# An attention block and a squared-ReLU feed-forward layer on one core: loads of the first pair reordered, transposes of the last queries in other PSUM banks, sums of W_in one step later

## The chip, the core and the metric

The kernel runs on one core of one Trainium2 chip. The metric is device time in microseconds of one execution. The times given are medians of several executions; the profile is of one execution, taken by the hardware profiler.

The engines are named as in the profile: PE is TensorE (PEld its weight loads), DVE is VectorE, ACT is ScalarE, POOL is GpSimd, and SP is the engine that issues nearly all DMAs here.

## The reference

```python
# q, k, v: (8, 8, 576, 64) float32; g_norm: (64,)
kv = np.einsum('bhsd,bhse->bhde', k, v)
out = np.einsum('bhsd,bhde->bhse', q, kv)
rms = np.sqrt(np.mean(out * out, axis=-1, keepdims=True) + 1e-06)
attn = out / rms * g_norm                      # (B, H, S, D)
x = attn.transpose(0, 2, 1, 3).reshape(4608, 512)
h = x @ w_in                                   # w_in: (512, 2048) float64
g = np.maximum(h, 0.0) ** 2
return (g @ w_out).astype(np.float32)          # w_out: (2048, 512) float64
```

The attention is linear: a key-value matrix of 64 x 64 for each batch and head, a product with the queries, a normalization per head. Then come an up product, relu squared, and a down product.

## The kernel before

**Tiling.** A batch b has 576 tokens of 8 heads. Heads go in pairs p = 0 to 3, so that a pair fills 128 columns. The tokens of a batch are four blocks of 128 (C = 4) and a rest of 64; the rests of two batches share one tile, so two batches make nine tiles of 128 tokens (PAIR). 36 tiles form nine strips s of four tiles (512 tokens). For each strip the kernel makes x, transposed (features on the partitions, `xt`), multiplies it by W_in (`up`), squares, and multiplies by W_out (`down`).

**Attention.** `load(b, p)` fetches k, v and q of a pair, `load_rest` the last 64 keys and values of all heads of a batch (k_rest, v_rest), `load_q_rest` the last queries. `key_value` (L347) multiplies keys by values into a PSUM tile kv_ps and copies two 64 x 64 blocks to SBUF with ACT (L357, L358). Its last two products take k_rest and v_rest. `transposed_query` (L322) makes qT: for b = 0 and 1 with PE transposes (L335) and a copy by ACT (L337), for later batches with DVE. For b = 1 it also transposes the last queries (L342) and copies them (L345). `query` multiplies qT by the key-value blocks (L386, x_ps), `normalized` scales (L427), and `features` transposes the result with PE (L473) for b < 2; later batches use DVE and DMAs. For b = 0 the first four tiles go another way: `first_queries` (L436), `first_normalized` (L443), `first_features` (L460), pair by pair, as soon as a pair has been loaded.

**Weights.** W_in and W_out come as float64 in 32 raw pieces of 512 KB (`load_piece`, L192, eight buffers). ACT takes the two halves of the words apart (L204, L207), DVE puts float32 together (L216 to L225). From the second strip on, the products use fewer, larger combinations of quarters (a scheme of seven products for a 2 x 2 block matrix), so sums of weights are needed: `sums_in(g)` scales a quarter of W_in by g_norm with ACT (L251, 128 x 2048) and makes four sums with DVE (L253, L242); `sums_out` does the like for W_out, and its results are stored to DRAM.

**Order.** All of it is written out by hand; each engine runs its instructions in program order. The opening is the list `slices` up to `ready[0]`: for each pair of b = 0 transposes T, key-values K, first queries Q, normalization N and features F, with raw pieces 0 to 3 converted in between. Then come, in strip 0, 16 steps `up_first` (i = 0 to 15, eight matmuls of 512 columns each), before each of which `convert(5 + (3*i + 2)//4)` emits conversions; in the last eight steps one slice of b = 1 follows each (T(1,0), K(1,0), T(1,1), ... K(1,3)). After them come 14 steps `down` (i = n_up to n_up + 13, p in the order 1, 2, 5, 6, 7, 3, 4, two steps each); the second of each pair ends with `combine`: for p = 1, 5, 6 ACT copies the bank (snap, L586), for p = 2, 7, 3 DVE adds bank and snap (L714), for p = 4 ACT copies the result (L712). Then strip 1 begins.

**Buffers.** PSUM has a pool with tag "at" (two banks: kv_ps, xt_ps) and tag "x" (one tile of two banks: t_ps, x_ps), and a pool with tags A (two banks), B and C (one each) for the up and down products. Before the change the transposed last queries lie in the second half of the kv_ps tile of the same pair (`kv_places`), so `key_value` of (1, p) writes to the bank from which L345 copies. q, k and v have two buffers each.

The order of loads at the start, as SP issues it before the change: k_rest, v_rest of b = 0; then for each pair k, v, q (q in two DMAs), with one raw piece after each pair from the second on; then more raw pieces. k_rest and v_rest are first cleared by DVE (L292, L293).

Of the kernel before, what the change touches and what calls it, by code (L numbers as in the profile page):

```python
# [10 lines left out]
FP32 = mybir.dt.float32  # L11
# [9 lines left out]
def kernel(  # L21
# [34 lines left out]
    nc = tc.nc  # L56
    P = 128
    B, H, S, D = q.shape
# [5 lines left out]
    C = S // P  # L64
# [32 lines left out]

    def load(b, p, q_eng):
        hs = slice(2 * p, 2 * p + 2)
        if b == 0 and p >= 2:  # L100

            h_place = g_pool.tile([P, 4, C * P], FP32, name="first_qkv", tag="gt")
        for i, (n, src, eng) in enumerate((("k", k, nc.sync), ("v", v, nc.sync), ("q", q, q_eng))):
            whole = src[b, hs, 0 : C * P].rearrange("h (sp c) d -> sp h c d", c=C)
            if n == "q" and b >= Q_ON_PE:

                t = qkv_pool.tile([P, 4 * C, SQ], FP32, name=n, tag=n)
                for a in range(4):
                    h, f = divmod(a * SQ, D)
                    eng.dma_start(  # L110
                        out=t[ts(a, SQ)],
                        in_=src[b, 2 * p + h, 0 : C * P, f : f + SQ].rearrange("(i k) f -> i k f", k=4 * C),
                    )
            elif n != "q":
                if b == 0 and p >= 2:
                    t = h_place[:, i].rearrange("p (h c d) -> p h c d", h=2, c=C)
                else:
                    t = qkv_pool.tile([P, 2, C, D], FP32, name=n, tag=n)
                eng.dma_start(out=t, in_=whole)
            else:  # L120

                if b == 0 and p >= 2:
                    t = h_place[:, i].rearrange("p (c h d) -> p c h d", h=2, c=C)
                else:
                    t = qkv_pool.tile([P, C, 2, D], FP32, name=n, tag=n)
                for h in range(2):
                    eng.dma_start(out=t[:, :, h, :], in_=whole[:, h])
            main[n, b, p] = t
# [9 lines left out]
    def load_rest(b, eng):  # L138
        h = b % 2
        half = slice(REST * h, REST * (h + 1))  # L140
        for t, src in ((k_rest[half], k), (v_rest[half, h], v)):
            eng.dma_start(out=t, in_=src[b, :, C * P : S].rearrange("h s d -> s h d"))
# [20 lines left out]
    def load_next(q_eng=nc.sync):  # L163
        u = next(to_load, None)
        if u is not None:
            load(*u, q_eng)
# [82 lines left out]
    def sums_in(g):  # L249

        nc.scalar.activation(w_in[:, :, g, 0:4], w_in[:, :, g, 0:4], AF.Copy, scale=g_col)  # L251
        a11, a21, a12, a22, s1, s2, s4 = (w_in[:, :, g, b] for b in range(7))
        nc.vector.tensor_tensor(out=s1, in0=a21, in1=a22, op=ALU.add)  # L253
        minus(nc.vector, s2, s1, a11)
        minus(nc.vector, s4, a12, s2)
        minus(nc.vector, a21, a11, a21)
# [39 lines left out]
    nc.vector.memset(one, 1.0)  # L296
    nc.scalar.sqrt(one, one)

    load_rest(0, nc.sync)
    load_next()  # L300
    for p in range(1, NP):
        load_next()
        load_piece()
# [13 lines left out]
            qT["rest", b // 2, p] = t[:, p]  # L317
        return t

    kv_places = {}  # L320

    def transposed_query(b, p):  # L322
        t = main.pop(("q", b, p))
        if b >= Q_ON_PE:
            qT[b, p] = qt_pool.tile([P, C, P], FP32, name="qT", tag="qT")
            nc.vector.transpose(out=flat(qT[b, p]), in_=flat(t))
            if b % 2 and p == NP - 1:
                nc.vector.transpose(
                    out=open_rest(b).rearrange("p q (k t) -> p q k t", k=4),
                    in_=squares(q_rest[b // 2]).rearrange("p k q f -> p q k f"),  # L330
                )
            return
        ps = apsum.tile([P, 2, C, P], FP32, name="t_ps", tag="x", bufs=1)[:, 0]
        for c in range(C):
            nc.tensor.transpose(ps[:, c, :], flat(t[:, c]), ident)  # L335
        qT[b, p] = qt_pool.tile([P, C, P], FP32, name="qT", tag="qT")
        nc.scalar.copy(qT[b, p], ps)  # L337
        if b % 2:
            t = q_rest[b // 2][:, 2 * p : 2 * p + 2]
            kv_places[b, p] = apsum.tile([P, 2 * P], FP32, name="kv_ps", tag="at")  # L340
            ps = kv_places[b, p][:, P : 2 * P]
            nc.tensor.transpose(ps, flat(t), ident)  # L342
            if p == 0:
                open_rest(b)
            nc.scalar.copy(qT["rest", b // 2, p], ps)  # L345

    def key_value(b, p):  # L347
        tk, tv = main.pop(("k", b, p)), main.pop(("v", b, p))

        place = kv_places.pop((b, p), None) or apsum.tile([P, 2 * P], FP32, name="kv_ps", tag="at")  # L350
        ps = place[:, 0:D]
        for c in range(C + 1):
            for h in range(2):
                a, w = (tk[:, h, c, :], tv[:, h, c, :]) if c < C else (k_rest[:, 2 * p + h], v_rest[:, b % 2, 2 * p + h])
                nc.tensor.matmul(ps[ts(h, D)], lhsT=a, rhs=w, start=c == 0, stop=c == C)  # L355
        d = kv_all[:, (NP * b + p) % (2 * NP + 1)]
        nc.scalar.copy(d[0:D, 0:D], ps[0:D])  # L357
        nc.scalar.copy(d[D:P, D:P], ps[D:P])  # L358
        kvd[b, p] = d
        if b < 2:  # L360
            if b == 1 and p < 2:
                load_next()
        else:
            load_next()
            if p == NP - 1 and b + 1 < B:
                load_rest(b + 1, nc.sync)
                load_q_rest(b + 1, nc.sync)
# [460 lines left out]
    for s in range(N_STRIP):  # L828
        attend(ready[s])
        if s == 0:  # L830
            steps = [(2, up_first, (g, fh, i)) for g in range(NG) for fh in range(2) for i in range(2)]
        else:
            steps = [(1, up, (s, g, p)) for g in range(NG) for p in ORDER]
        n_up = len(steps)
        if s < DEEP:

            steps += [(2, down, (s, p, i)) for p in (ORDER if s else (1, 2, 5, 6, 7, 3, 4)) for i in range(2)]
        else:
            steps += [(2, down_deep, (s, k, i)) for k in range(7) for i in range(2)]
        goal = ready.get(s + 1, len(slices))  # L840
        total, done = sum(w for w, _, _ in steps), 0
        for i, (w, fn, a) in enumerate(steps):
            if s == 0 and i < n_up:

                convert(5 + (3 * i + 2) // 4)
                if i in (2, 4):
                    load_next()
                if i == 3:
                    load_q_rest(0, nc.sync)
                    load_rest(1, nc.sync)  # L850
                    load_q_rest(1, nc.sync)
            elif s == 0 and i == n_up:
                convert(len(conversions))
                conv.close()
                sum_pool = ctx.enter_context(tc.tile_pool(name="sum", bufs=8, reuse_waits="tile"))
                c_pool = ctx.enter_context(tc.tile_pool(name="c", bufs=6, reuse_waits="tile"))
                stream_pool = ctx.enter_context(tc.tile_pool(name="stream", bufs=4, reuse_waits="tile"))
                stream(3)
                for b, t in enumerate(w_first):
                    for e in range(2):  # L860
                        nc.sync.dma_start(out=w_out[b, :, e], in_=t[:, :, ts(e, P)])
            if s == 0 and n_up <= i < n_up + NG:
                sums_g(0, i - n_up)
            fn(*a)
            done += w
            if s:
                attend(ready[s] + int((goal - ready[s]) * min(done / (0.42 * total), 1)))
                if s >= DEEP and i == n_up - 3:
                    leaf_sums(s, 4)
                if s == DEEP - 1 and i == len(steps) - 1:  # L870
                    sums_x(s + 1)
                    stream(4)
                continue
            if i in (n_up + 4, n_up + 5):
                load_next()
            if i == n_up + 6:
                load_rest(2, nc.sync)
                load_q_rest(2, nc.sync)
            if i - n_up in (6, 8, 10, 12):
                sums_in((i - n_up - 6) // 2)  # L880
            if i == n_up + 9:
                sums_x(1)

            n_kv = ready[0] + 2 * NP
            if i < n_up:
                attend(ready[0] + max(0, (i + 1) - n_up + 2 * NP))
            else:
                attend(n_kv + (goal - n_kv) * min(i + 1 - n_up, 6) // 6)
# [30 lines left out]
```

## Time and profile before

| what | us |
|---|---|
| median of 5 runs | 949.53 (947.12 to 950.23) |
| the five runs | 947.5, 947.12, 950.23, 949.61, 949.53 |
| profiled execution | 947.5, span 945.7 |
| PE busy in 0 to 35 us | 17.57 |
| PE busy in 35 to 68.6 us | 33.57 of 33.60 |
| PE busy in 68.6 to 98.9 us | 27.57 of 30.30 |
| PE busy in 98.9 to 152.6 us | 53.02 of 53.70 |
| PE busy in 152.6 to 260 us | 104.03 of 107.40 |
| PE busy in 260 to 946 us | 680.36 of 686.00 |

How to read it: the span is the time from the first to the last instruction in the trace. "Busy" is the time in which an engine runs an instruction. A row of the timeline gives start, duration, engine, line, operation, written and read tiles with their shapes; in square brackets stand the idle time of the engine just before it and what ended that idle time. A row of waits gives the waiting engine and line, the releaser, the total in us, the number of waits and the longest. PEclk is the granted PE clock, 1.00 being full speed. In the first 35 us PE works half of the time; from there to the end it is busy almost without a break.

### The profile page before, as it was taken

The numbers are of one execution on the slowest core, as the hardware profiler recorded it, in microseconds if no ns is written. First come the engines' busy times: TensorE is split into PE (matmuls) and PEld (weight loads), VectorE is DVE, ScalarE is ACT, GpSimd is POOL, SyncE is SP. The second block draws the span as 40 slices with busy tenths as digits, with TensorE's granted clock in tenths as the row PEclk, the third lists the DMA queues.
The fourth block names the chain that finished last, engine by engine and source line by source line (L and its number), as shares of the span: only waits on it lengthen the run. The fifth ranks groups of instructions, "written<-read, shape, count | busy, mean of one in ns | idle before, by whom it ended". The sixth has DMA issues, their size and how long they took to land.

```text
span 945.7 us, 17026 instructions
## 1 busy us (share of the span) xinstructions
PE 916.1 (97%) x6880; PEld 805.2 (85%) x6880; DVE 658.1 (70%) x1147; ACT 226.7 (24%) x494; POOL 1.7 (0%) x7
## 2 busy tenths in 40 slices
PE   4799999999999999999999999999999999999998
PEld 4434788888788998899989998899889988998898
DVE  3999754586436896489737975598559854983496
ACT  3797341320023102210122012200320022002200
POOL 0000000000000000000000000000000000000000
PEclk9999999999999999999999999999999999999999
DMA  8799882537866486648654874477516831682075
GB/s 257 249 292 306 272 238 106 131 99 255 294 230 151 150 309 199 149 139 290 230 143 119 299 259 128 113 277 256 158 46 222 309 95 65 219 297 75 1 257 178
DMA packets 164287, 185.94 MB, mean 197 GB/s; under 512 B 83953, under 2 KB 137713, under 8 KB 155633
## 3 DMA queue, kind: packets, MB, share of 16 engines
q1 hardware_dynamic: 163888, 184.72, 61.5%
q8 instruction: 54, 0.88, 0.4%
q14 instruction: 25, 0.20, 0.1%
q10 hardware_dynamic: 320, 0.13, 0.1%
HBM read 153.62 MB, written 31.20 MB: 195 GB/s over the span
## 4 chain that ended last, share of the span: by engine, by line
PE 89%; DMA 4%; DVE 3%; ACT 3%; issue 1%; SPq 0%; DVEq 0%; ACTq 0%
PE ps_A L576 30%; PE ps_B L761 18%; PE ps_B L576 14%; PE ps_A L761 13%; PE ps_C L576 7%; PE kv_ps L355 2%; PE x_ps L386 2%; ACT raw L207 1%; DMA w_blk<-w_out 1%; ACT w_c L204 1%; DMA w_blk<-w_deep 1%; DMA raw<-in_moe_w_out_dram 1%; PE ps_A L612 1%; DVE w_c L222 1%; DMA q<-in_q_dram 0%
## 5 line engine op out<-in xcount | busy, mean ns | idle before, releaser
L576 PE MATMUL ps_A<-x_t,w_in 128*128 128x256 f32 x768 | 183.2, 381 | 0.0
L576 PEld LDWEIGHTS ps_A<-x_t,w_in 128*128 128x128 f32 x768 | 144.4, 190 | 20.3 <-ACT snap L586 0.3
L761 PE MATMUL ps_B<-w_blk,g_s 128*128 128x128 f32 x896 | 109.2, 275 | 0.0
L761 PEld LDWEIGHTS ps_B<-w_blk,g_s 128*128 128x128 f32 x896 | 104.6, 192 | 0.0
L761 PE MATMUL ps_B<-w_blk,gt 128*128 128x128 f32 x672 | 84.3, 275 | 0.1
L761 PE MATMUL ps_A<-w_blk,g_s 128*128 128x128 f32 x672 | 81.9, 275 | 0.0
L761 PEld LDWEIGHTS ps_B<-w_blk,gt 128*128 128x128 f32 x672 | 80.1, 192 | 0.7 <-DMA w_blk<-w_deep 0.3
L761 PEld LDWEIGHTS ps_A<-w_blk,g_s 128*128 128x128 f32 x672 | 78.4, 192 | 0.0
L635 DVE TENSOR_TENSOR gt<-ps_A,snap 128x512 f32<-128x512 f32 x32 | 22.1, 691 | 74.0 <-PE ps_A L576 74.0
L586 ACT COPY snap<-ps_A 128x512 f32<-128x512 f32 x68 | 39.9, 586 | 134.9 <-PE ps_A L576 128.5
L635 DVE TENSOR_TENSOR gt<-ps_C,snap 128x512 f32<-128x512 f32 x32 | 22.1, 689 | 69.8 <-PE ps_C L576 69.8
L636 DVE SCALAR_TENSOR_TENSOR gt<-gt 128x512 f32<-128x512 f32 x96 | 66.4, 692 | 3.3
L761 PE MATMUL ps_A<-w_blk,gt 128*128 128x128 f32 x504 | 63.1, 275 | 0.0
L576 PE MATMUL ps_A<-xT,w_in 128*128 128x256 f32 x256 | 61.3, 382 | 0.0
L576 PE MATMUL ps_C<-xT,w_in 128*128 128x256 f32 x256 | 61.1, 381 | 0.0
L576 PE MATMUL ps_B<-x_t,w_in 128*128 128x256 f32 x256 | 61.0, 381 | 0.0
L576 PE MATMUL ps_B<-xT,w_in 128*128 128x256 f32 x256 | 61.0, 381 | 0.0
L242 DVE TENSOR_TENSOR gt<-gt 128x2048 f32<-128x2048 f32 (+1 forms) x31 | 58.1, 1874 | 4.0 <-PE ps_C L576 3.8
L761 PEld LDWEIGHTS ps_A<-w_blk,gt 128*128 128x128 f32 x504 | 59.7, 192 | 0.0
L576 PEld LDWEIGHTS ps_B<-x_t,w_in 128*128 128x128 f32 x256 | 48.2, 190 | 6.7
L576 PEld LDWEIGHTS ps_B<-xT,w_in 128*128 128x128 f32 x256 | 48.2, 190 | 6.7
L576 PEld LDWEIGHTS ps_C<-xT,w_in 128*128 128x128 f32 x256 | 48.1, 190 | 6.7
(116 smaller groups left out, 1170.3 us busy)
## 6 DMA issues: line engine op xcount, KB each, us to landing
w_blk<-w_deep SPq DMA_DIRECT2D x49, 1024.0 KB, 5.5
w_blk<-w_out SPq DMA_DIRECT2D x49, 768.0 KB, 5.2
w_blk<-w_out SPq DMA_DIRECT2D x11, 1024.0 KB, 6.9
raw<-in_moe_w_in_dram SPq DMA_DIRECT2D x16, 512.0 KB, 6.1
raw<-in_moe_w_out_dram SPq DMA_DIRECT2D x16, 512.0 KB, 5.6
k<-in_k_dram SPq DMA_DIRECT2D x30, 256.0 KB, 3.0
v<-in_v_dram SPq DMA_DIRECT2D x30, 256.0 KB, 3.4
w_deep<-w_t SPq DMA_DIRECT2D x7, 1024.0 KB, 8.4
```

Of the source, the lines that this page charges most:

```text
L204: nc.scalar.activation(c, high_f, AF.Abs)
L207: nc.scalar.activation(r, low, AF.Copy, scale=2.0**-29)
L222: yield nc.vector.scalar_tensor_tensor(out=ci, in0=high, scalar=-(2**30), in1=ci, op0=ALU.bitwise_and, op1=ALU.bitwise_or)
L242: eng.tensor_tensor(out=out, in0=a, in1=b, op=ALU.subtract)
L355: nc.tensor.matmul(ps[ts(h, D)], lhsT=a, rhs=w, start=c == 0, stop=c == C)
L386: nc.tensor.matmul(ps[half, r, i, ts(p, D)], lhsT=q[row, half], rhs=kvd[b, p][row, row], start=True, stop=True)
L576: nc.tensor.matmul(bank[BANK[p]][:, i, :], lhsT=lhsT(k), rhs=rhs(k), start=p in (1, 5, 2) and i == 0 and k == 0, stop=k == n - 1, skip_gro ...
L586: nc.scalar.copy(snap[p], b)
L612: nc.tensor.matmul(ps, lhsT=w_in[:, kc % KH, g, kc // KH * 2 + fh, ts(i, P)], rhs=xt[0][:, :, kc, :], start=kc == 0, stop=kc == NP - 1,)
L635: nc.vector.tensor_tensor(out=o, in0=b, in1=a, op=ALU.add)
L636: nc.vector.scalar_tensor_tensor(out=o, in0=o, scalar=0.0, in1=o, op0=ALU.max, op1=ALU.mult)
L761: nc.tensor.matmul(chain[c][x][:, i, :], lhsT=a[:, f, :], rhs=w[:, f, :], start=p not in (6, 7, 3) and j in ((1, 2) if place(s, p) is LAST ...
```

## The change

There are four edits.

1. **Loads of b = 0.** `load` takes q first, then k, v for b = 0 (later batches keep k, v, q), and `load_next()` of the first pair stands ahead of `load_rest(0)`.
2. **Banks of the transposes.** `t_ps`, the PE transposes of the queries of b = 0 and 1, moves from tag "x" to tag "at". The transposed last queries of b = 1 move from the kv_ps tile to a tile of their own with tag "x" (tr_ps), and kv_ps shrinks to 64 columns. `kv_places` goes.
3. **Last tokens of b = 0 and 1.** `load_q_rest(0)`, `load_rest(1)` and `load_q_rest(1)` are called at up step 2 instead of 3.
4. **Sums of W_in.** `sums_in(0)` to `sums_in(3)` are called after down steps 7, 9, 11, 13 instead of 6, 8, 10, 12, so after the `combine` of p = 6, 7, 3 and 4 instead of before it.

```diff
--- before.py
+++ after.py
@@ -97,10 +97,11 @@
 
     def load(b, p, q_eng):
         hs = slice(2 * p, 2 * p + 2)
+        inputs = (("q", q, q_eng), ("k", k, nc.sync), ("v", v, nc.sync))
         if b == 0 and p >= 2:
 
             h_place = g_pool.tile([P, 4, C * P], FP32, name="first_qkv", tag="gt")
-        for i, (n, src, eng) in enumerate((("k", k, nc.sync), ("v", v, nc.sync), ("q", q, q_eng))):
+        for i, (n, src, eng) in enumerate(inputs if b == 0 else inputs[1:] + inputs[:1]):
             whole = src[b, hs, 0 : C * P].rearrange("h (sp c) d -> sp h c d", c=C)
             if n == "q" and b >= Q_ON_PE:
 
@@ -296,8 +297,8 @@
     nc.vector.memset(one, 1.0)
     nc.scalar.sqrt(one, one)
 
+    load_next()
     load_rest(0, nc.sync)
-    load_next()
     for p in range(1, NP):
         load_next()
         load_piece()
@@ -316,8 +317,6 @@
         for p in range(NP):
             qT["rest", b // 2, p] = t[:, p]
         return t
-
-    kv_places = {}
 
     def transposed_query(b, p):
         t = main.pop(("q", b, p))
@@ -330,15 +329,14 @@
                     in_=squares(q_rest[b // 2]).rearrange("p k q f -> p q k f"),
                 )
             return
-        ps = apsum.tile([P, 2, C, P], FP32, name="t_ps", tag="x", bufs=1)[:, 0]
+        ps = apsum.tile([P, C, P], FP32, name="t_ps", tag="at")
         for c in range(C):
             nc.tensor.transpose(ps[:, c, :], flat(t[:, c]), ident)
         qT[b, p] = qt_pool.tile([P, C, P], FP32, name="qT", tag="qT")
         nc.scalar.copy(qT[b, p], ps)
         if b % 2:
             t = q_rest[b // 2][:, 2 * p : 2 * p + 2]
-            kv_places[b, p] = apsum.tile([P, 2 * P], FP32, name="kv_ps", tag="at")
-            ps = kv_places[b, p][:, P : 2 * P]
+            ps = apsum.tile([P, 2, C * P], FP32, name="tr_ps", tag="x", bufs=1)[:, 0, 0:P]
             nc.tensor.transpose(ps, flat(t), ident)
             if p == 0:
                 open_rest(b)
@@ -347,8 +345,7 @@
     def key_value(b, p):
         tk, tv = main.pop(("k", b, p)), main.pop(("v", b, p))
 
-        place = kv_places.pop((b, p), None) or apsum.tile([P, 2 * P], FP32, name="kv_ps", tag="at")
-        ps = place[:, 0:D]
+        ps = apsum.tile([P, D], FP32, name="kv_ps", tag="at")
         for c in range(C + 1):
             for h in range(2):
                 a, w = (tk[:, h, c, :], tv[:, h, c, :]) if c < C else (k_rest[:, 2 * p + h], v_rest[:, b % 2, 2 * p + h])
@@ -845,7 +842,7 @@
                 convert(5 + (3 * i + 2) // 4)
                 if i in (2, 4):
                     load_next()
-                if i == 3:
+                if i == 2:
                     load_q_rest(0, nc.sync)
                     load_rest(1, nc.sync)
                     load_q_rest(1, nc.sync)
@@ -876,8 +873,8 @@
             if i == n_up + 6:
                 load_rest(2, nc.sync)
                 load_q_rest(2, nc.sync)
-            if i - n_up in (6, 8, 10, 12):
-                sums_in((i - n_up - 6) // 2)
+            if i - n_up in (7, 9, 11, 13):
+                sums_in((i - n_up - 7) // 2)
             if i == n_up + 9:
                 sums_x(1)
 
```

In the built program the instructions of PE keep their order. On SP the first loads change places as told. On ACT one L251 moves from before the snap of p = 6 to after it, and the last one from before the copy of p = 4 (L712) to after it. On DVE the two additions L714 of p = 7 and p = 3 each come one set of sums earlier.

## The prediction

> **What bounds the kernel now.** I read the page first (busy shares, slices, chain), then the waits of TensorE (PE), then the timeline around each wait that the change touches, then the DMA landings in narrow windows.
>
> ```profile
> span 945.7 us, 17026 instructions
> PE 916.1 (97%) x6880; PEld 805.2 (85%) x6880; DVE 658.1 (70%) x1147; ACT 226.7 (24%) x494; POOL 1.7 (0%) x7
> PE   4799999999999999999999999999999999999998
> PE 89%; DMA 4%; DVE 3%; ACT 3%; issue 1%; SPq 0%; DVEq 0%; ACTq 0%
> ...
> PE t_ps L335 <- DMA q<-in_q_dram: 9.7, 1, 9.7
> PE kv_ps L355 <- ACT qT_rest L345: 2.7, 1, 2.7
> PE xt_ps L473 <- DVE x_n L427: 1.1, 1, 1.1
> PE ps_A L576 <- ACT snap L586: 0.7, 1, 0.7
> ```
>
> PE is the bound after the second slice; it has 29.6 us of idle (945.7 - 916.1), most of it in the first 35 us. Only what shortens the opening, or one of the few later PE waits, can move the end. The four waits shown are those that the change comes near. The rest of the 946 us is queued behind PE, and I found no later wait with a clock of its own: the two w_blk waits (0.4 at 245 us, 1.9 at 254 us) follow DMAs that are issued as PE frees buffers. So a shift won by 150 us should reach the end.
>
> The timeline of the stall that the second part removes:
>
> ```profile
> 64.80 0.33 PE L342 MATMUL kv_ps<-ident,q_rest 128*128 128x128 f32 x1
> 64.97 3.61 PE L612 MATMUL ps_B<-xT,w_in 128*128 128x512 f32 x8
> ...
> 70.95 0.27 ACT L345 COPY qT_rest<-kv_ps 128x128 f32<-128x128 f32 x1
> 71.27 0.69 PE L355 MATMUL kv_ps<-v,k 128*64 128x64 f32 x16 [2.69 <-ACT qT_rest L345]
> 72.00 5.40 PE L612 MATMUL ps_A<-xT,w_in 128*128 128x512 f32 x8
> ...
> 90.60 0.68 ACT L204 ACTIVATE w_c<-raw 128x512 f32<-128x512 f32 x1 [2.49 <-DMA raw<-in_moe_w_out_dram]
> 95.47 0.19 ACT L357 COPY kv_all<-kv_ps 64x64 f32<-64x64 f32 x1
> 98.15 0.69 PE L355 MATMUL kv_ps<-v,k 128*64 128x64 f32 x16
> ```
>
> PE stands 2.69 us because the copy L345 is far down ACT's queue (ACT is busy with the weight conversions), and the next up product runs 5.40 us instead of 3.60. Note the ACT row at 90.60, which waits for a raw W_out piece.
>
> **What the Trainium skill says.** "PSUM — Partial Sum Buffer", section "PSUM bank collisions raise a hardware error": accesses must be guarded by bank, not by address. That is why L355 waits for L345 although they use other columns of the bank; the 2.69 us agree. "TensorE: Matmul & The Clock Gate", Part 1, "What's actually happening": the PE clock halves after an idle window of about 3.4 us and returns after a busy one, and the windows run free. The trace agrees: granted clock 0.50 to 0.54 in 31 to 34 us and 72 to 75 us, each after an idle of over 2.3 us, and Q(0) takes 2.04 us where later Q(p) take 1.16. PSUM page, "Engine vs sequencer instructions": ACT and DVE queues are strict FIFO; so the order on them decides parts 2 and 3. The trace agrees: the rest transpose ends at 65.1 and its copy L345 runs at 70.95, after everything that stands before it in the program.
>
> **Part 1, loads.** Before, SP issues k_rest, v_rest, k, v, q; the first waits for DVE's memset of k_rest (L292) and starts at 1.42 us. After, q (two DMAs), k, v come first and need no memset; SP is ready at about 0.75. In narrow DMA windows q lands 4.0 to 4.4 us after issue, k 4.1, v 4.0. So PE can start near 5 us, not 9.75: 4 to 5 us at the first transpose. But most of that is not on the path. ACT's queue holds the conversion of raw piece 0 (L204 at 15.35) ahead of the copy qT(0,1), and raw 0, issued 8.32, landed 6.9 us later, at 15.2. ACT thus stands at raw 0, whatever PE does. Raw 0 comes behind the same DMAs as before; it gains the 0.67 us of the memset wait, about 0.3 of the v_rest wait, and the hole in the DMA near 4 us: I take 1.0 (0.7 to 1.4). Raw 1 (landed 18.8, used 19.16) and raw 2 (22.6, 23.55) follow with it.
> Against this: PE will be done with K(0,1) at about 13.8 and cannot start Q(1) before act(0), the copy qT and the copies kv, near 16.4. The 2.6 us idle can leave the clock halved: Q(1) 2.04 for 1.16, a loss of 0.88 on the chain Q(1) - square - DVE, which takes nearly all of the 1.0. If the clock returns only after Q(2), the sum is about -0.5. Bounds +1.0 and -0.5; I take +0.7, since the five times before (947.1 to 950.2) suggest that the profiled run had a kind clock and the median one had not.
> The moves of banks for b = 0 (t_ps now in "at", two banks shared with kv_ps) wait for copies that lie a whole pair back: nothing. q_rest and the rests at i = 2 instead of 3: no DMA is issued between, SP's order is the same: nothing.
>
> **Part 2, transposes of b = 1.** The built program shows that L355 of (1,0) loses its ACT wait; in return T(1,p) waits for the copy qT(1,p-1), the rest transpose for the copy L345(1,p-1), and K(1,p) for the copies kv(1,p-1). I walk PE with warm times (up product 3.43, T with rest 0.55, K 0.9) against ACT's old times:
> K(1,0) 68.6, product to 72.9, T(1,1) (copy done 71.1), product to 76.9, K(1,1) (copies kv(1,0) end 76.8: just free), product to 81.2, T(1,2) (copies end 81.2 and 81.4: 0.2 lost), product to 85.4, K(1,2) (83.3), product, T(1,3), product to 93.8. PE is 4.3 us ahead here. K(1,3) then needs the copies kv(1,2), rows L357/L358, at 95.47 to 95.88. These follow in ACT's queue the conversion of raw 31, issued 85.7, landed 92.8, issued late because its buffer is freed by DVE at 84.4. None of that depends on PE. So K(1,3) goes at 95.95 instead of 98.15: 2.2 us gained, 2.1 given back to a new wait. Next, x_ps L386 comes at 100.35 and needs kv(1,3), about 100.0: free. The slow 5.40 us product costs nothing extra, as PE met ACT again at 81.4. Ends: 4.3 if ACT too runs earlier, 1.0 if ACT runs later or the new 2.1 us idle halves the clock. I take 2.2.
>
> **Part 3, sums of W_in.** Four scales L251 (2.02 us each, pitch 1.89) and 16 DVE sums move one step. The snap at 131.14 waited for PE, not for L251 (ACT idle 4.32), so PE's 0.68 us behind it stays: no gain. The fourth L251 falls behind the copy L712 (152.85), thus from 153.3 to 155.35, and its DVE sums (2.65 us) stand ahead of the strip-1 work:
>
> ```profile
> 152.85 0.59 ACT L712 COPY o_sb<-ps_A 128x512 f32<-128x512 f32 x1 [15.44 <-PE ps_A L576]
> 154.53 0.59 ACT L586 COPY snap<-ps_A 128x512 f32<-128x512 f32 x1 [1.10 <-PE ps_A L576]
> 156.33 0.69 DVE L635 TENSOR_TENSOR gt<-ps_C,snap 128x512 f32<-128x512 f32 x1 [7.09 <-PE ps_C L576]
> 160.87 0.69 DVE L427 TENSOR_TENSOR x_n<-x_ps,rms 128x512 f32<-128x512 f32 x1 [0.47 <-PE ps_B L576]
> 161.62 0.66 PE L473 MATMUL xt_ps<-ident,x_n 128*128 128x128 f32 x4 [1.12 <-DVE x_n L427]
> ```
>
> The snap of 154.53 slips to 155.2, harmless (PE's next ps_A is at 156.78). L635 slips from 156.33 to 158.1. Then L636 158.8, L398 159.4, L399 160.15, root on ACT 160.4, Newton to 161.4, L427 161.5 for 160.87. PE already waits for x_n, so 0.65 us is pure loss; if L427's odd 0.36 us wait stays, 1.0 to 1.15. I take 0.7. Behind L635 also wait o_sb stores, which nobody is short of.
>
> **Sum.** Against the profiled execution, 947.5 (span 945.7 and 1.8 around it): -0.7 - 2.2 + 0.7 = -2.2, i.e. 945.3. That execution lies 2.0 below the median of the five; I carry the difference to the median: 949.5 - 2.2 = 947.3.
>
> **Rivals.** (B) The clock is warm at Q(1) in most runs and ACT runs a little earlier at 95: parts 1 and 2 give 1.4 and 3.0: 945.8. For it: raw 0 gains up to 1.4; against it: the idle before Q(1). (C) The gain is eaten: part 1 gives -0.5, part 2 about 1.5, part 3 costs 1.1: 949.6, no change. For it: ACT and DVE are 94 to 100% busy from 35 to 68 us, and the same raw pieces rule. (D) Slower: the halved clock in the opening. Place: Q(1) to Q(3), 16.4 to 28 us; price: 0.88 for each Q, 1.0 for each T and K, 0.88 + 1.9 + 1.9 = 4.7 us at most, less the 1.0 of earlier raws. It decides once the opening loses 3.4 us net (2.2 - 0.7 + 1.9): 949.5 - 1.5 + 3.7 = 951.7. Against it: a window holding 14.0 to 17.4 us, 86% busy, sufficed before to bring the clock back.
>
> **How the numbers follow.** About 0.2% (1.9 us) is what a measurement of this kernel can tell from no change. Forecast 947.3 (own range 946.2 to 948.3) 0.54, of which 0.14 above 947.6; B 0.20; C 0.14; D 0.12. Faster 0.40 + 0.20 = 0.60, same 0.28, slower 0.12. The range, 945.2 to 950.2, takes in B and C and leaves out D and the tail of B.
>
> **What would show it.** First transpose near 5 us, L204 of raw 0 near 14.3; Q(1) of 2.0 us or 1.2; no wait of L355 on L345, but one of about 2 us of the last L355 on L358; a PE wait for x_n at strip 1 of 1.8 us or more instead of 1.1; the fourth L251 behind L712. I am wrong if raw 0 lands no earlier, if K(1,3) is not held by ACT, or if a wait after 160 us takes the shift back.

## The result and the profile after

| kernel | median us | lowest to highest | runs |
|---|---|---|---|
| before | 947.28 | 944.48 to 950.74 | 80 |
| changed | 945.0 | 940.81 to 947.98 | 43 |

The ratio of changed to before is 0.9973, with a 95% interval of 0.9966 to 0.998. Of 947.28 us that is 2.6 us less (1.9 to 3.2; the two medians lie 2.3 apart). A second set of 22 runs beside 36 of before gave 0.9971 (0.9959 to 0.9982). So the change makes the kernel slightly, but measurably, faster. The forecast of the difference was 2.2 us. The forecast of the time, 947.3, was 2.3 us too high and the lower end of the range, 945.2, lay 0.2 above the result, because the kernel before is 2.25 us faster in 80 runs than in the five that the forecast started from.

The profiled execution of the changed kernel took 944.69 us. From its page: span, PE's busy time, and the chain that ended last.

```profile
span 942.9 us, 17026 instructions
PE 915.5 (97%) x6880; PEld 805.0 (85%) x6880; DVE 658.2 (70%) x1147; ACT 226.6 (24%) x494; POOL 1.7 (0%) x7
PE 87%; DVE 4%; DMA 4%; ACT 3%; issue 1%; SPq 0%; DVEq 0%; ACTq 0%
```

PE's busy time is nearly what it was (915.5 for 916.1) and the span is 2.8 us shorter, so it is idle time that went. The waits of PE in the changed kernel (line, releaser, total us, times, longest):

```profile
PE t_ps L334 <- DMA q<-in_q_dram: 4.9, 1, 4.9
PE kv_ps L352 <- ACT kv_all L355: 2.8, 1, 2.8
...
PE xt_ps L470 <- DVE x_n L424: 1.7, 1, 1.7
PE ps_A L573 <- ACT snap L583: 0.7, 1, 0.7
```

Against the four lines shown of before: the first transpose waits 4.9 us and not 9.7; the wait for the copy of the last queries (2.7) is gone, and a wait for the copies of keys-values (2.8) has come in its place; the wait for x_n has grown from 1.1 to 1.7; the one for snap has stayed. The timeline of the changed kernel shows the places (start, duration, engine, line, operation, tiles, and in brackets the idle time before and what ended it):

```profile
4.86 1.09 PE L334 MATMUL t_ps<-ident,q 128*128 128x128 f32 x4 [4.86 <-DMA q<-in_q_dram]
...
11.80 0.60 ACT L392 ACTIVATE sq<-x_ps 128x512 f32<-128x512 f32 x1 [2.23 <-PE x_ps L433]
12.79 0.68 ACT L205 ACTIVATE w_c<-raw 128x512 f32<-128x512 f32 x1 [0.39 <-DMA raw<-in_moe_w_in_dram]
...
14.86 1.16 PE L433 MATMUL x_ps<-kv_all,qT 128*128 128x128 f32 x8 [1.48 <-ACT kv_all L355]
...
65.82 0.69 PE L352 MATMUL kv_ps<-v,k 128*64 128x64 f32 x16
...
90.73 0.66 ACT L205 ACTIVATE w_c<-raw 128x512 f32<-128x512 f32 x1 [1.07 <-DMA raw<-in_moe_w_out_dram]
...
93.49 0.21 ACT L355 COPY kv_all<-kv_ps 64x64 f32<-64x64 f32 x1
...
93.75 0.69 PE L352 MATMUL kv_ps<-v,k 128*64 128x64 f32 x16 [2.83 <-ACT kv_all L355]
...
94.48 5.41 PE L573 MATMUL ps_A<-w_in,gt 128*128 128x256 f32 x16
99.82 0.34 PE L383 MATMUL x_ps<-kv_all,qT_rest 64*64 64x64 f32 x8
...
159.46 0.66 PE L470 MATMUL xt_ps<-ident,x_n 128*128 128x128 f32 x4 [1.68 <-DVE x_n L424]
```

Four rows of the kernel before, from the same two places:

```profile
14.86 0.60 ACT L395 ACTIVATE sq<-x_ps 128x512 f32<-128x512 f32 x1 [2.22 <-PE x_ps L436]
15.35 0.66 ACT L204 ACTIVATE w_c<-raw 128x512 f32<-128x512 f32 x1
...
98.88 3.72 PE L576 MATMUL ps_A<-w_in,gt 128*128 128x256 f32 x16
102.53 0.34 PE L386 MATMUL x_ps<-kv_all,qT_rest 64*64 64x64 f32 x8
```

PE starts 4.9 us earlier, but ACT's conversion of raw piece 0 only 2.6 us (12.79 for 15.35). What holds this conversion has changed: before, ACT stood 2.22 us for PE's first product x_ps, squared it, and converted raw 0 right behind, without a wait of its own; now ACT is through with the square earlier and stands 0.39 us for raw 0. At 65.82 the key-values of (1,0) start with no wait. At 93.75 the last key-values, of (1,3), stand behind L355, which follows the conversion of a raw W_out piece that had to land first (row 90.73). They start 4.4 us earlier than before (98.15), but the down product after them takes 5.41 us where before it took 3.72 (row 98.88). So x_ps stood at 102.53 before and stands at 99.82 now: 2.7 us gained. The longer wait for x_n takes 0.56 of it back. The 2.2 us that are left at the transposes of x_n (159.46 for 161.62) reach the end of the kernel.

### The profile page after: what moved, and what is told of

The parts are those of the page before. It is cut to its first block, busy times and chain, and to the rows that moved or that the text cites. A ratio compares the mean times of both kernels' runs of the same rounds, so it can differ in the third digit from the quotient of the medians.

```text
span 942.9 us, 17026 instructions
## 1 busy us (share of the span) xinstructions
PE 915.5 (97%) x6880; PEld 805.0 (85%) x6880; DVE 658.2 (70%) x1147; ACT 226.6 (24%) x494; POOL 1.7 (0%) x7
## 4 chain that ended last, share of the span: by engine, by line
PE 87%; DVE 4%; DMA 4%; ACT 3%; issue 1%; SPq 0%; DVEq 0%; ACTq 0%
PE ps_A L573 30%; PE ps_B L758 18%; PE ps_A L758 14%; PE ps_B L573 14%; PE ps_C L573 7%; PE kv_ps L352 2%; PE x_ps L383 2%; DMA raw<-in_moe_w_out_dram 2%; DMA w_blk<-w_out 1%; ACT w_c L205 1%; ACT raw L208 1%; DVE w_c L223 1%; DMA raw<-in_moe_w_in_dram 1%; DMA k_rest<-in_k_dram 0%; DVE w_in L226 0%
## 5 line engine op out<-in xcount | busy, mean ns | idle before, releaser
L632 DVE TENSOR_TENSOR gt<-ps_A,snap 128x512 f32<-128x512 f32 x32 | 22.1, 691 | 73.6 <-PE ps_A L573 73.6
L583 ACT COPY snap<-ps_A 128x512 f32<-128x512 f32 x68 | 39.9, 586 | 135.7 <-PE ps_A L573 122.2
L632 DVE TENSOR_TENSOR gt<-ps_C,snap 128x512 f32<-128x512 f32 x32 | 22.1, 690 | 62.7 <-PE ps_C L573 62.7
```

Of the source, the lines that this page charges most:

```text
L583: nc.scalar.copy(snap[p], b)
L632: nc.vector.tensor_tensor(out=o, in0=b, in1=a, op=ALU.add)
```

## The experiments

Three theories were to be told apart. Theory A is the forecast's: the earlier raw 0 gives a little, the transposes in other banks give about 2 us and meet a new wait, the later sums cost 0.7. Its rivals: the loads carry the gain and the banks give theirs back through the new wait and the halved clock behind it; or the five-run median was simply not the level of the kernel before. Every ratio below is to runs of the kernel before on the same chip, and brackets are 95% intervals.

**1. The loads alone.** The edits of `load` and of the first pair's place, on the kernel before:

```diff
+        inputs = (("q", q, q_eng), ("k", k, nc.sync), ("v", v, nc.sync))
-        for i, (n, src, eng) in enumerate((("k", k, nc.sync), ("v", v, nc.sync), ("q", q, q_eng))):
+        for i, (n, src, eng) in enumerate(inputs if b == 0 else inputs[1:] + inputs[:1]):
...
-    load_rest(0, nc.sync)
     load_next()
+    load_rest(0, nc.sync)
```

> Only the loads of the change (q first, first pair ahead of the last tokens); banks and sums as before. Theory (the opening's gain is carried by everything behind it): raw piece 0 is converted at about 12.8 us instead of 15.35, the whole chain of ACT and DVE is 2.6 us early, and so is the PE stall on the rest copy (L355 on L345): still about 2.7 us long, but it ends near 68.7 instead of 71.3. Time against before: -2.6 us (ratio 0.9972). Rival (the gain of the opening is hidden by the weight conversions, the banks carry the change): -1.0 us or less (0.999 or more).

Measured: 0.9984 [0.9975, 0.9993], or 1.5 us less. Raw 0 was converted at 13.83. The stall on the copy of the last queries was still there with 2.10 us, and the wait for x_n with 1.10. So this part gives twice what the forecast gave it. The 2.6 us of the theory above lie outside the interval, the 1.0 of its rival inside. Of the 1.5 us that raw 0 gained in this profile, 1.0 was left at the first up product (31.16 for 32.17) and 0.6 at the end of the stall (70.66 for 71.27).

**2. The place of the rests alone.** Only the two lines at the end of the diff above; k, v, q in the old order:

> Only load_rest moved behind the first pair; order k, v, q kept; banks and sums as before. Theory (the memset wait and the earlier issue carry the opening; the place of q within a pair matters only for the first transpose): raw 0 lands near 12.8 us, -2.6 us as with all the loads. Rival (q first matters, because it changes which transfers fly beside raw 0): raw 0 lands near 14.3 us, -1.0 us.

Measured: 0.9983 [0.9975, 0.999]. The first transpose came at 6.38 and not near 4.6, and the time is the same as with q first. Whether PE starts at 6.4 or at 4.6 does not matter: ACT waits for raw 0 at its conversion in both kernels (0.75 us here, 1.72 in experiment 1). What counts is the place of the rests. It also moves PE's start away from the path: in all four profiles with the rests first, ACT stood 2.22 or 2.23 us for the first x_ps, and in three of them it converted raw 0 right behind the square, raw 0 having landed 0.1 to 1.2 us earlier. No run moves PE's start or raw 0 alone. With them behind the first pair SP issues its first DMA at 0.73 us and not at 1.42, when DVE has cleared k_rest.

**3. The banks alone.** The edits of t_ps, tr_ps and kv_ps, as in the change:

> Only the banks of the transposes; loads and sums as before. Theory: the last L355 (pair 3 of b = 1) starts at 96 instead of 98.15, after a new wait of about 2.1 us on the copies of pair 2 (L358); where that wait halves the PE clock for the next product, 1.7 us of the 2.2 are lost again. Time -0.5 (clock halved, 0.9995) to -2.2 us (not halved, 0.9977). Rival (the removed stall and its slow product are won whole, 2.69 + 1.8): -4.4 us (0.9954).

Measured: 0.9982 [0.9971, 0.9993], 1.7 us less, which leaves out the 4.4 us of the rival. The timeline around the last key-values of batch 1 in this kernel:

```profile
93.88 0.68 ACT L204 ACTIVATE w_c<-raw 128x512 f32<-128x512 f32 x1 [0.81 <-DMA raw<-in_moe_w_out_dram]
...
96.70 0.21 ACT L354 COPY kv_all<-kv_ps 64x64 f32<-64x64 f32 x1
...
96.96 0.69 PE L351 MATMUL kv_ps<-v,k 128*64 128x64 f32 x16 [1.85 <-ACT kv_all L354]
...
97.69 3.72 PE L572 MATMUL ps_A<-w_in,gt 128*128 128x256 f32 x16
```

The new wait appears without the new loads, so it belongs to the banks. Here the clock was not halved behind it: 3.72 us for the product. In this execution the first up product began 1.07 us later than in the profile of before (33.24 for 32.17), and the last key-values 1.19 earlier (96.96 for 98.15), so between the two places it won 2.3 us.

**4. The sums alone.** The edit of the four steps, as in the change:

> Only the sums of W_in one step later; loads and banks as before. Theory: the wait of PE for x_n in strip 1 grows from 1.1 to about 1.7 us, nothing else moves: +0.6 us (1.0006). Rival (the copy ahead of the sums lets PE go on earlier): the 0.68 us wait of PE on the snap of p = 6 goes, -0.5 us.

Measured: 1.0004 [0.9995, 1.0012]. The time cannot tell 0.6 us from nothing, but the trace can. The transposes of x_n in this kernel:

```profile
155.75 0.69 PE L386 MATMUL x_ps<-kv_all,qT 64*64 64x64 f32 x32
...
161.77 0.65 PE L473 MATMUL xt_ps<-ident,x_n 128*128 128x128 f32 x4 [1.67 <-DVE x_n L427]
```

From x_ps to the transposes it is 6.02 us, for 5.47 before (156.15 to 161.62), and the wait is 1.67 for 1.12. The sums cost 0.55 us at this place.

The three parts give -0.0016, -0.0018 and +0.0004, together -0.0030, and the whole change -0.0027 [-0.0034, -0.0020]: within the intervals they add up.

**5. The changed kernel with the sums put back.**

```diff
-            if i - n_up in (7, 9, 11, 13):
-                sums_in((i - n_up - 7) // 2)
+            if i - n_up in (6, 8, 10, 12):
+                sums_in((i - n_up - 6) // 2)
```

> The changed kernel with the sums of W_in put back to their old steps (6, 8, 10, 12). Theory: the wait for x_n is 1.1 us again instead of 1.7, so 0.6 us faster than the changed kernel: -3.1 us against before (0.9967). Rival (the later sums help somewhere else): the same as the changed kernel or slower, 0.9973 or more.

Measured: 0.9965 [0.9952, 0.9978], 0.0008 lower than the change but not apart from it. The wait for x_n is back at 1.10, and from x_ps to the transposes it is 5.45 us. In this execution the new wait on keys-values was 1.59 and the product behind it took 3.72.

**6. The wait filled with work.** To keep PE busy where it stands, six products of 128x512 whose results are overwritten were put ahead of the last key-values:

```diff
     def key_value(b, p):
         tk, tv = main.pop(("k", b, p)), main.pop(("v", b, p))
+        if (b, p) == (1, 3):
+            opened["A"] = fpsum.tile([P, 2, 2 * P], FP32, name="ps_A", tag="A", bufs=2)
+            for _ in range(6):
+                nc.tensor.matmul(flat(opened["A"]), lhsT=ident, rhs=xt[0][:, :, 0, :], start=True, stop=True)
```

> The changed kernel with six extra matmuls of 128x512 (ident by xT, about 2.6 us, the result is not used) on PE just ahead of the last L352 (pair 3 of b = 1), in the bank that the next down product opens. They fill the wait on the copies of pair 2 and change no data. Theory (the wait halves the PE clock, which costs 1.7 us): the last L352 starts when it did, the next product takes 3.7 us instead of 5.4, so more work makes the kernel 1.7 us faster than the changed one: -4.2 us against before (0.9955). Rival (the slow product is work for the bank or for ACT, not the clock): no gain, or up to 2.6 us lost, 0.9973 to 1.000.

Measured: 0.9992 [0.9981, 1.0002]; the timeline of this kernel says why:

```profile
92.96 5.31 PE L353 MATMUL ps_A<-xT,ident 128*128 128x512 f32 x12
98.20 0.69 PE L358 MATMUL kv_ps<-v,k 128*64 128x64 f32 x16
...
98.94 3.72 PE L579 MATMUL ps_A<-w_in,gt 128*128 128x256 f32 x16
```

The six products stand in the trace as twelve matmuls of 0.44 us and take 5.31 us, twice the 2.6 that were expected and longer than the wait that they were to fill. The clock stayed up, but the filler delays what it should help: the run shows what too much work there costs, and nothing on the theory.

**7. The same with two products** (`range(2)`), and beside it on the same chip **8. the changed kernel once more.**

> The changed kernel with two additional 128x512 products, whose results are overwritten, ahead of the last keys-values of batch 1; six of them took 5.31 us, so two should take about 1.8 us of the 2.83 us that TensorE stands there. Clock theory (the idle 2.83 us halves the clock, and the next product then takes 5.41 instead of 3.72): the last keys-values start where they did, at 93.5 to 94.5 us, with a wait of about 1.0, the next product takes 3.7 us; the ratio to before is 0.9955 to 0.9975, up to 1.7 us better than the changed kernel beside it, by as much as its clock is halved in the timed runs. Rival (the 5.41 us were of that one profile, and the clock in the timed runs is mostly full there): the same ratio as the changed kernel's beside it, within 0.0006.

> The changed kernel as it is, beside the other two on the same chip. Both theories: 0.9966 to 0.998 to before, as measured first. Opening theory: raw piece 0 is converted at 12.7 to 14.0 us, the rest transposes wait for nothing, the last keys-values of batch 1 wait 1.5 to 2.9 us for the copies of keys-values. If the clock theory holds, a profile with a wait of under 2 us there shows 3.7 us for the next product, one of over 2.5 us shows 5.4.

Measured: 0.9958 [0.9947, 0.9969] with two products, 0.9971 [0.9959, 0.9982] without. The difference, 1.2 us, points to the clock theory, but the intervals overlap. The timeline with two products, then that of the changed kernel in its second profile:

```profile
92.32 1.88 PE L353 MATMUL ps_A<-xT,ident 128*128 128x512 f32 x4
95.38 0.69 PE L358 MATMUL kv_ps<-v,k 128*64 128x64 f32 x16 [1.18 <-ACT kv_all L361]
...
96.11 3.72 PE L579 MATMUL ps_A<-w_in,gt 128*128 128x256 f32 x16
```

```profile
15.04 2.08 PE L433 MATMUL x_ps<-kv_all,qT 128*128 128x128 f32 x8 [1.44 <-ACT kv_all L355]
...
94.45 0.69 PE L352 MATMUL kv_ps<-v,k 128*64 128x64 f32 x16 [1.29 <-ACT kv_all L355]
...
95.18 3.72 PE L573 MATMUL ps_A<-w_in,gt 128*128 128x256 f32 x16
```

The very same kernel shows 5.41 us for this product in one profile and 3.72 in the other. In the second it had lost its microsecond in the opening: Q(1) took 2.08 and not 1.16 us, PE came later to the last key-values, and waited there 1.29 and not 2.83 us (1.5 to 2.9 were expected). That a wait of under 2 us leaves the next product at 3.7 came as expected in both profiles, and in that of experiment 5. How often the clock is halved at 94 us in the timed runs stays open.

**9. The last key-values one step later.** The wait can be removed at its root: the last key-values and all that follows them of batch 1 go behind the first down product, on the changed kernel:

```diff
-                attend(ready[0] + max(0, (i + 1) - n_up + 2 * NP))
+                attend(ready[0] + min(max(0, (i + 1) - n_up + 2 * NP), 2 * NP - 1))
+            elif i == n_up:
+                attend(n_kv)
             else:
-                attend(n_kv + (goal - n_kv) * min(i + 1 - n_up, 6) // 6)
+                attend(n_kv + (goal - n_kv) * min(i - n_up, 6) // 6)
```

> The changed kernel with the last key-values of b = 1 and all queries of b = 1 called one down step later, so that a down product of 3.6 us stands where PE waits for the copies of pair 2. Theory: wait and halved clock both go (2.8 + 1.7 us), the next need, x_ps for the copies of pair 3, is met too: 4.4 us faster than the changed kernel, -6.9 us against before (0.9927). Rival (ACT's chain is the bound and the wait reappears one step on, at x_ps or at the transposes L470): at most 1.7 us faster than the changed kernel, -4.2 us or less (0.9955 or more).

Measured: 0.995 [0.9933, 0.9968], median 941.71. The timeline of this kernel:

```profile
91.18 3.62 PE L573 MATMUL ps_A<-w_in,gt 128*128 128x256 f32 x16
94.73 0.69 PE L352 MATMUL kv_ps<-v,k 128*64 128x64 f32 x16
...
95.46 3.72 PE L573 MATMUL ps_A<-w_in,gt 128*128 128x256 f32 x16
```

No bracket stands in these rows: PE goes from the up products through a down product into the key-values and on, at full clock, and no wait of this size comes in its place later. The time is some 2 us better than that of the change (0.9971 and 0.9973), though the intervals still touch. The 4.4 us of the theory (0.9927) lie outside the interval, and the bound of the rival (0.9955) inside: in time the shift gives half of what the wait and the slow product of one profile promised. The profiled execution, 938.11, is the lowest of the kernel's seven timed ones. The first up product took 3.60 us in it (5.29 in the first profile of the changed kernel), and the wait for w_blk near 254 us, 1.9 in the kernel before and 2.0 in the changed one, is 0.3; so the profile flatters it.

**10. The same shift on the kernel before.**

> The kernel before, with the last key-values and the queries of b = 1 one down step later; loads, banks and sums as before. A control: there PE does not wait at the last L355 (98.15 us), since it has lost its time at the stall of the first one. Theory: nothing to fill, so no change, -0.3 to +0.3 us (0.9997 to 1.0003). Rival (the order alone is the better one, by starting the down products earlier): -2 us or more (0.998 or less).

Measured: 0.9991 [0.9982, 1.0]. In the trace of this kernel the stall on the copy of the last queries was there with 2.02 us, and the product behind it took 5.40:

```profile
72.04 0.69 PE L355 MATMUL kv_ps<-v,k 128*64 128x64 f32 x16 [2.02 <-ACT qT_rest L345]
...
72.77 5.40 PE L612 MATMUL ps_A<-xT,w_in 128*128 128x512 f32 x8
```

The shift pays about 0.9 us here (0 to 1.7), more than the 0.3 expected and less than the 2 of the rival, and about 2 us on the changed kernel. The two gains differ by less than their intervals. That the shift takes away the new wait, which the banks brought, is shown by the trace of experiment 9 and not by the times.

**11. Later key-values and the old place of the sums.** Experiments 9 and 5 together:

> The changed kernel with the last keys-values and queries of batch 1 one down step later, as in the run before that did best (0.995), and the sums of W_in at their old place. If the later sums cost what the traces show (0.6 us at the wait for x_n), the ratio is 0.9943, and the wait for x_n is 1.1 us or less; TensorE waits nowhere between 60 and 129 us. Rival: with TensorE about 6 us earlier, the sums stand in VectorE's way at their old place as well, the wait for x_n stays at 1.6 and the ratio at 0.995 or above.

Measured: 0.9948 [0.9929, 0.9968], median 941.55. The wait for x_n is 0.75 us, so the rival (that the sums stand in the way at their old place too, once PE is earlier) fell. The time cannot be told from that of experiment 9. These two are the best versions found.

## Why the prediction was right and wrong

**The level: the step that failed.** The prediction said: "That execution lies 2.0 below the median of the five; I carry the difference to the median: 949.5 - 2.2 = 947.3." The profiled execution, 947.5, was an ordinary one. It was the median of the five that lay high: 80 runs of before gave 947.28, and the groups beside the experiments 946.91, 946.97 and 947.48. With 947.28 the same sum gives 945.1, and 945.0 was measured. The same mistake stands in part 1, where the five times were taken as a sign that the profiled run had a kind clock. The range had no term for the level of the kernel before, although its five times spread by 3.1 us.

**The sum of the change** was forecast at -2.2 and measured at -2.6 [-3.2, -1.9]. That it came out so near is in part luck: part 1 gave 0.8 more than forecast, part 2 0.5 less, and part 3 cost 0.3 less. Its three terms:

*Part 1, forecast -0.7, measured -1.5 [-2.4, -0.7].* The first transpose gains 4.9 us, and most of it is lost again at ACT, as forecast. But the step "ACT thus stands at raw 0, whatever PE does" was wrong for the kernel before: there ACT stood for PE's first x_ps (rows 14.86 and 15.35 above), and raw 0 had landed by then, at 15.2. PE's late start and raw 0 came almost together, PE last. With the rests behind the first pair the step is right: ACT waits for raw 0 in eight of nine profiles, 0.39 to 1.82 us.

Too small, therefore, was the term "I take 1.0 (0.7 to 1.4)" for raw 0, which counted its landing alone. In the nine profiles with the rests behind the first pair its conversion starts at 12.71 to 14.01, mean 13.38; in the four without, at 14.80 to 15.52, mean 15.25. That is 1.9 us. Raw 0 itself lands 1.4 us earlier (mean 13.3 for 14.8): it is issued 0.8 earlier (7.5 for 8.3) and is some 0.7 less on its way. The other 0.4 had been lost to PE. The windows of the opening, first of before and then of the changed kernel, show what changes on that way (stretch, its length, busy us and instructions of PE, PEld, DVE, ACT, POOL, then the clock, the DMA share and GB/s):

```profile
0.00:3.00 3.00, 0.00 (x0) 0.00 (x0) 1.41 (x3) 1.49 (x2) 1.70 (x7) 1.00 0.00 0
3.00:6.00 3.00, 0.00 (x0) 0.00 (x0) 0.00 (x0) 0.00 (x0) 0.00 (x0) 1.00 0.66 135
```

```profile
0.00:3.00 3.00, 0.00 (x0) 0.00 (x0) 1.41 (x3) 1.49 (x2) 1.70 (x7) 1.00 0.20 45
3.00:6.00 3.00, 1.09 (x4) 0.72 (x4) 0.00 (x0) 0.02 (x1) 0.00 (x0) 1.00 0.82 239
```

In the first 6 us the DMA engines move 3 x 135 = 405 KB before and 3 x (45 + 239) = 852 KB after. The first issue is 0.7 us earlier, and the pair's large transfers come ahead of the rests; no run separates the two. That less stands in the queue ahead of raw 0 when it is issued would explain its shorter way; this is argued, not tested.

The counterweight, a halved clock at Q(1), was real. With the new place of the rests, seven of nine profiles have a Q(1), Q(2) or Q(3) of 1.33 us or more (2.08 in the second profile above), of the four others one. So of the 1.9 us only 1.6 arrive at the first up product: mean start 30.54 (nine profiles) for 32.16 (four). The forecast took off 0.3 for it.

*Part 2, forecast -2.2, measured -1.7 [-2.7, -0.7].* The walk of PE held. The changed kernel's first profile reaches the last key-values at 90.92 (93.75 - 2.83), before at 98.15. That is 7.2 us, of which 3.0 came with the first up product (29.14 for 32.17): 4.2 from this part, for 4.3 forecast (4.6 if one counts from the up product ahead of the stall, at 62.29 for 64.97). That the copies of keys-values behind a raw piece then end last is confirmed too, in experiment 3 by itself. They hardly follow PE, as the forecast said: the products that they copy came 7.3 us earlier (82.50 for 89.78), the copies 2.2 (93.70 for 95.88). The loads moved them as well: with the new loads the last key-values start at 93.75 to 95.67 in the four profiles that wait there, with the banks alone at 96.96, so parts 1 and 2 add. The bound "the new 2.1 us idle halves the clock" came true in one of the two profiles of the changed kernel: 5.41 - 3.72 = 1.7 us.

*Part 3, forecast +0.7, measured +0.55 in the trace* (experiments 4 and 5), 0.4 [-0.5, 1.1] in the time. The path was the one worked out. In the timeline of the changed kernel:

```profile
150.62 2.00 ACT L252 ACTIVATE w_in<-w_in,g_col 128x2048 f32<-128x2048 f32 x1
...
152.65 0.69 DVE L254 TENSOR_TENSOR w_in<-w_in 128x512 f32<-128x512 f32 x1 [6.13 <-ACT w_in L252]
153.38 2.02 DVE L243 TENSOR_TENSOR w_in<-w_in 128x512 f32<-128x512 f32 x3
...
155.32 0.68 DVE L632 TENSOR_TENSOR gt<-ps_C,snap 128x512 f32<-128x512 f32 x1
...
158.72 0.69 DVE L424 TENSOR_TENSOR x_n<-x_ps,rms 128x512 f32<-128x512 f32 x1
```

The last scaling (L252) ends at 152.62, behind the copy of o_sb. DVE, which had stood idle for 6.13 us, then has four sums to do, and only after them the strip's own work: L632 starts at 155.32, though its snap (L583) ended at 153.10 and its product in ps_C by 153.5. DVE queues in program order: the prediction named the Trainium skill's "PSUM — Partial Sum Buffer", "Engine vs sequencer instructions" for that, and this trace agrees. The snap, which the edit was to free from the scale, still costs PE 0.68 us, since it waits for PE.

**What was put at nothing.** The opening's transposes in "at": no profile of the changed kernel shows a PE wait for a copy there. The rests of b = 0 and 1 at step 2 were not tried alone. SP issues the same DMAs in the same order with them, and the three parts account for the whole without them. The first transpose of the last queries waited 0.3 to 1.4 us for its own DMA in four of six profiles with step 3 and in two of seven with step 2; whether the step has a part in that stays open.

**The rivals.** B gave 945.8 from parts 1 and 2 with 1.4 and 3.0. Its time lies closest to the one measured, but its difference, 3.7 us, lies outside the interval (1.9 to 3.2), so it came near by luck, from a level that was too high. C (no change) and D (slower) fell: a halved clock in the opening costs about 1 us (experiment 3 has a Q(1) of 2.08 us and its first up product 1.07 us later than before), not 4.7, and in no profile was more than one of Q(1) to Q(3) slowed all through.

**Open:** how often the clock is halved at 94 us, and so how much of the 2 us of experiment 9 is the wait and how much the clock; and how much of part 1 PE's earlier start would give without an earlier raw 0.

## What to carry to other kernels

Before carrying a difference to a level, ask how well the level is known: five runs that spread by 3 us leave their median open by as much as the change was worth here. When a wait is taken from a filled engine, walk on to the next thing it will meet, and look whether that can be moved behind independent work: here the wait removed (2.0 to 2.7 us) was replaced by another one (1.3 to 2.8), and one step of reordering removed that too. When two things that release an engine come within tenths of each other, don't call one of them off the path: the engine stands until the later one, and moving the other alone gives nothing. At the start of a kernel, look at what stands at the head of the load queue and what that waits for: here the first weight piece landed 1.4 us later for it.

## What was not expected of the hardware

- The length of an idle time alone does not decide the clock. In the opening Q(1) took 1.16 us after 2.39 us of idle in experiment 9, and 2.08 after 1.44 in experiment 8. After the opening the waits nearly sort by length: in the thirteen profiles no wait of up to 2.00 us left slow work behind it, and all four of 2.10 to 2.83 did. At the edge 1.99 us left the next product at 3.70 (experiment 4, rows below), 2.02 made it 5.40 (experiment 10), and 2.04, ahead of a product on w_blk in experiment 1, left it at its usual 7.14. The Trainium skill's "TensorE: Matmul & The Clock Gate", Part 1, "What's actually happening", says that the windows run free of the program and that the same kernel varies with their phase. These runs agree (the same kernel has a Q(1) of 1.16 us after 1.48 of idle in its first profile and of 2.08 after 1.44 in its second), and put a price on it: about 1 us a time in the opening and 1.7 us at a product of 3.7. The idle window of about 3.4 us, with which the prediction said that the trace agrees, is not what these runs show as a lower limit: shorter waits were enough, 2.69 us in the profile of before. Rows of experiment 9, then of experiment 4:

```profile
16.07 1.16 PE L433 MATMUL x_ps<-kv_all,qT 128*128 128x128 f32 x8 [2.39 <-ACT kv_all L355]
```

```profile
71.06 0.69 PE L355 MATMUL kv_ps<-v,k 128*64 128x64 f32 x16 [1.99 <-ACT qT_rest L345]
...
71.79 3.70 PE L612 MATMUL ps_A<-xT,w_in 128*128 128x512 f32 x8
```

- The recorded clock reads 1.00 in the first 15 us of both kernels, while the first product x_ps takes 2.04 us and later ones 1.16. The durations show the slow start, the clock column doesn't.
- A float32 product of 128x512 is two matmuls in the trace and took 0.89 us (5.31 us for six).
